# Spare matmuls with zero weights into an open PSUM accumulation, and a shorter window for the planner that places them

## Chip, cores, metric

One core of one Trainium2 chip. The metric is the device time of one execution in microseconds (us), median of the runs. The experiments ran in three sets, each on another chip, beside the kernel before on the same one.

## The reference

Two layers, each of multi-head attention and an MLP, on x of 2048 rows by 512, in bf16. Attention has 32 heads of 16; the MLP has 1792 hidden columns and a tanh gelu.

```python
x = x + A(layernorm(x), wqkv, wo)        # softmax(q k^T / 4) v, 32 heads of 16, then wo
x = x + B(layernorm(x), w1, b1, w2, b2)  # gelu(x w1 + b1) w2 + b2
x = x + A(layernorm(x), wqkv, wo)
x = x + B(layernorm(x), w1, b1, w2, b2)
```

## The kernel before

A Python planner runs before anything is compiled. It has a model of each engine's time, picks the next operation for each engine, and so fixes every engine's instruction order and its semaphores (the counters by which one engine waits for another). The 4096 score tiles (128 keys by 512 queries, one PSUM bank each) are the core of the work: ScalarE takes the exp of most of them, two or three banks at a time, VectorE approximates the exp of the rest, and TensorE multiplies the result with V ("PV") into bank 5, which stays open through a pass of the keys.

By its trace TensorE is idle for 199.6 of the 1629.9 us of the span, and its granted clock was 0.50 after windows of 3.41 us in which it had been idle. So the planner puts *spare matmuls* into gaps. Their results are never read. In the code below, shortened, `...` stands for what is cut, as is a guard in the `for` line.

```python
WINDOW = 3.4      # us over which the planner averages its estimate of TensorE's activity
WARM = 0.38       # below this average, a gap gets spare matmuls
...
    def fill(self, start, nxt):            # before TensorE's next operation, due at `start`
        while self.filler and self.mode:
            now = self.clock["pe"]
            mode = "F" if nxt.mode == self.mode == "F" else "P"
            into, back = ...               # the planner's cost of changing the tiling, 0.107 us each
            b, t = self.free(now, nxt.writes)   # which bank is free, and when
            now = max(now, t)
            if start - now < into + MM + back + FMARGIN or self.active(start) >= WARM:
                return
            op = self.filler(b, mode)      # four matmuls of 32 columns side by side: one group
            ...
    def free(self, now, ahead):
        best = (None, 1e9)
        for b in (6, 7, 0, 1, 2, 3, 4, 5):
            k = "B.%d" % b
            if k in ahead or not P.reads.get(k) and P.lastw.get(k) not in self.s.fills:
                continue                   # still holds a result that someone has to read
            t = ...                        # when its last reader is done
            if max(t, now) < max(best[1], now):
                best = (b, t)
        return best
```

So a gap gets nothing if no bank's last reader is done in time. The 0.107 us is a constant of the planner. In the trace before, a PV group starts 0.32 or 0.33 us after the score group ahead of it (329.75 and 330.08, 331.05 and 331.37), and 0.21 or 0.22 us after another PV group (330.09, 330.30, 330.52), so the change from one to the other took about 0.1 us there.

The softmax here doesn't subtract the row's maximum and nothing guards it: scores larger than these inputs give would overflow.

## Time and profile before

| | before |
|---|---|
| median of the first 3 runs | 1632.78 us |
| span in the profile | 1629.9 us |
| ScalarE busy / idle | 1560.7 / 69.2 us |
| mean granted TensorE clock, profiled run | 0.986 |
| windows of 3.41 us at half clock in that run | 13 |
| groups of spare matmuls | 174 on free banks |

ScalarE (ACT) is the bound: with the exps and the gelus above all it is busy for 96% of the span. What can be won lies in its idle time, and about half of that is the kernel's start and end. The lines that carry this are shown in the prediction.

### The profile page before, as it was taken

The page shows a single profiled execution, that of the slowest core. Times are in us where ns is not written, and L with a number is a line of the kernel's source. Part 1 is how long each engine was busy: PE and PEld are TensorE (multiplying, and loading weights), DVE is VectorE, ACT ScalarE, POOL GpSimd, SP SyncE. Part 2 cuts the span into 40 slices and gives each one's busy share as a digit, 9 for nine tenths or more (in the row PEclk, how much of TensorE's full clock was granted, in tenths as well). Part 3 has the DMA queues.
Part 4 walks back from the last instruction along what each step waited for, and adds up shares of the span by engine and source line. Part 5 has one row for each costly group of instructions (what it writes and reads, how often), then busy time and mean ns, then how long its engine had stood idle before and what let it go on. Part 6 is the DMA issues. An engine that isn't in the chain of part 4 may idle for free.

```text
span 1629.9 us, 32720 instructions
## 1 busy us (share of the span) xinstructions
PE 1430.3 (88%) x13701; PEld 418.1 (26%) x13838; DVE 1355.2 (83%) x2612; ACT 1560.7 (96%) x1402; POOL 111.6 (7%) x143
## 2 busy tenths in 40 slices
PE   6997888989898989899889989788898889888988
PEld 2222222222222222222222222222222222233434
DVE  6579999878887988987787788888888988897883
ACT  5999999999999999999998999989999999999995
POOL 3200000000000000000110001111000000000000
PEclk9999999999999999999999999999999999999999
DMA  5100001001010011100111001001101100010110
GB/s 173 22 1 1 1 14 34 27 4 39 25 33 27 1 27 40 34 27 1 27 46 47 7 14 40 2 1 27 46 11 30 34 14 11 17 40 24 50 53 27
DMA packets 88319, 44.85 MB, mean 28 GB/s; under 512 B 33645, under 2 KB 88174, under 8 KB 88174
## 3 DMA queue, kind: packets, MB, share of 16 engines
q1 hardware_dynamic: 88174, 42.75, 9.8%
q8 instruction: 111, 1.82, 0.5%
q14 instruction: 34, 0.28, 0.1%
HBM read 33.03 MB, written 2.10 MB: 22 GB/s over the span
## 4 chain that ended last, share of the span: by engine, by line
ACT 58%; PE 36%; DVE 3%; issue 1%; DMA 1%; POOL 0%; ACTq 0%
ACT pt L1360 49%; PE ps L1064 11%; PE ps L1421 11%; PE ps L868 4%; ACT v L1360 4%; PE ps L822 4%; PE ps L638 3%; ACT g L855 3%; ACT kt L1360 2%; PE ps L635 1%; DVE du L1209 1%; PE ps L749 1%; PE ps L1051 1%; ACT L855 1%; DMA xf<-xln 1%
## 5 line engine op out<-in xcount | busy, mean ns | idle before, releaser
L1360 ACT ACTIVATE pt<-ps 128x1024 bf16<-128x1024 f32 (+1 forms) x1217 | 1335.7, 1244 | 30.2 <-PE ps L1064 14.4
L1064 PE MATMUL ps<-qp,kt 32*128 32x512 bf16 x4096 | 545.5, 387 | 149.6 <-ACT pt L1360 109.5
L1209 DVE TENSOR_SCALAR du<-ps 128x512 uint16<-128x512 f32 x650 | 440.1, 685 | 112.7 <-PE ps L1064 106.2
L1421 PE MATMUL ps<-pt,v 128*17 128x512 bf16 (+1 forms) x3205 | 450.9, 364 | 2.3 <-ACT pt L1360 1.0
L1064 PEld LDWEIGHTS ps<-qp,kt 32*128 32x128 bf16 x4096 | 141.9, 91 | 700.6 <-ACT pt L1360 304.1
L1421 PE MATMUL ps<-du,vc 128*17 128x512 bf16 (+1 forms) x2178 | 305.1, 360 | 1.6 <-DVE du L1272 1.1
L1272 DVE TENSOR_SCALAR du<-du 128x2048 uint16<-128x2048 uint16 (+1 forms) x329 | 222.4, 681 | 2.5
L1028 POOL TENSOR_SCALAR qp<-q,mask 128x512 bf16<-128x512 bf16 (+1 forms) x92 | 68.7, 747 | 1273.0 <-PE ps L1064 1263.7
L1421 PE MATMUL ps<-du,v 128*17 128x512 bf16 (+1 forms) x726 | 140.3, 363 | 2.4 <-DVE du L1272 0.9
L1421 PEld LDWEIGHTS ps<-pt,v 128*17 128x17 bf16 x3205 | 107.6, 88 | 125.8 <-issue 96.7
L1270 DVE TENSOR_SCALAR du<-du 128x1024 uint16<-128x1024 uint16 (+1 forms) x329 | 136.6, 424 | 2.6
L868 PE MATMUL ps<-w,g 128*128 128x512 bf16 x404 | 118.5, 396 | 9.6 <-issue 5.7
L822 PE MATMUL ps<-xf,wr 128*128 128x512 bf16 (+1 forms) x427 | 111.0, 362 | 7.5 <-issue 5.6
L1360 ACT ACTIVATE v<-ps 128x1536 bf16<-128x1536 f32 (+1 forms) x77 | 102.6, 1354 | 4.0 <-PE ps L1421 2.0
L1421 PE MATMUL ps<-dh,vc 128*17 128x512 bf16 (+1 forms) x369 | 105.5, 360 | 0.1
L1421 PEld LDWEIGHTS ps<-du,vc 128*17 128x17 bf16 x2178 | 83.0, 89 | 58.5 <-issue 26.5
L836 DVE TENSOR_SCALAR g<-ps,hb1t 128x512 bf16<-128x512 f32 (+1 forms) x112 | 79.9, 713 | 16.8 <-PE ps L822 15.1
L1209 DVE TENSOR_SCALAR dh<-ps 128x512 uint16<-128x512 f32 x111 | 76.2, 686 | 12.1 <-PE ps L1064 9.2
L1209 DVE TENSOR_SCALAR kt<-ps 128x512 uint16<-128x512 f32 x98 | 67.3, 686 | 15.8 <-PE ps L1064 14.6
L1051 PE MATMUL ps<-w 128*32 128x512 bf16 x697 | 71.5, 398 | 1.8 <-DVE du L1209 1.6
L1360 ACT ACTIVATE kt<-ps 128x1536 bf16<-128x1536 f32 (+1 forms) x52 | 71.6, 1382 | 0.7 <-PE ps L1064 0.3
L1421 PE MATMUL ps<-kt,v 128*17 128x512 bf16 (+1 forms) x264 | 63.1, 365 | 0.1
(78 smaller groups left out, 1136.1 us busy)
## 6 DMA issues: line engine op xcount, KB each, us to landing
wr<-in_B_w_dram SPq DMA_DIRECT2D x59, 256.0 KB, 2.9
wr<-in_A_wqkv_dram SPq DMA_DIRECT2D x24, 256.0 KB, 2.8
wr<-in_A_wo_dram SPq DMA_DIRECT2D x18, 256.0 KB, 2.9
x<-in_A_x_dram SPq DMA_DIRECT2D x4, 512.0 KB, 8.5
out_dram<-x SPq DMA_DIRECT2D x16, 128.0 KB, 1.7
w<-in_B_w_dram SPq DMA_DIRECT2D x1, 1792.0 KB, 11.0
g<-in_A_wqkv_dram SPq DMA_DIRECT2D x3, 512.0 KB, 6.2
kt<-in_B_w_dram SPq DMA_DIRECT2D x4, 256.0 KB, 3.3
```

The source lines that it names most:

```text
L822: fns = [lambda e, dc=dc, j=j, pb=pb: e.matmul(pb, lhsT=T["WR"][w][:, 256 * dc + 128 * j:256 * dc + 128 * j + 128], rhs=T["XF"][:, dc, q], ...
L836: yield _Op("dve", 0.21 + n / 966, lambda e, fc=fc, pb=pb: e.tensor_scalar(T["G"][:, fc, q], pb, T["HB1T"][:, fc:fc + 1], None, op0=ALU.ad ...
L855: fns.append(lambda e, g=g: e.activation(out=g, in_=g, func=ACT.Gelu_apprx_tanh))
L868: fns = [lambda e, fc=fc: e.matmul(pb, lhsT=T["G"][:, fc, q], rhs=T["W2"][:, fc, :], start=(fc == 0), stop=False) for fc in range(NFC)]
L1028: yield _Op("pool", 0.1 + 0.6 * w / 512, lambda e, s=s, q=q, i=i, t=t, w=w: e.tensor_scalar(T["QP"][:, s, w * i:w * i + w], q, T["MASK"][: ...
L1051: fns.append(lambda e, o=o, a=a, m=m: e.matmul(o, lhsT=T["W2"][:, 0, m * a:m * a + m], rhs=T["W2"][:, 1, :], start=True, stop=True, tile_p ...
L1064: return (lambda e: e.matmul(o, lhsT=lhsT, rhs=rhs, start=True, stop=True, tile_position=(32 * a, 0)), ["K%d.%d.%d" % (l, gb, kt // 4), "Q ...
L1209: yield _Op("dve", 0.68, lambda e: e.tensor_scalar(u, self.bank(b), E_SCALE, E_BIAS, op0=ALU.mult, op1=ALU.add), reads=["B.%d" % b], write ...
L1270: yield _Op("dve", 0.08 + 0.14 * n, lambda e: e.tensor_scalar(U[:, 1, 0:n, :], U[:, 0, 0:n, :], SHIFT, None, op0=ALU.add), reads=key[0], w ...
L1272: yield _Op("dve", 0.08 + 0.28 * n, lambda e: e.tensor_scalar(U[:, 2:4, 0:n, :], U[:, 0:2, 0:n, :], 2 * SHIFT, None, op0=ALU.add), reads=k ...
L1360: yield _Op("act", 0.065 + 0.4267 * n, lambda e, src=src, dst=dst: e.activation(out=dst, in_=src, func=ACT.Exp, scale=0.25), reads=["B.%d" ...
L1421: op.fns.append(lambda e, o=o, lhsT=q[0][0][m], rhs=q[0][1][:, n * m:n * m + n], a=a, st=st, sp=sp: e.matmul(o, lhsT=lhsT, rhs=rhs, start= ...
```

## The change

The intent: when no free bank can be had at once, spare matmuls go to bank 5 in the midst of its accumulation, with weights of zero, which are meant to leave the sums as they are; and the planner averages activity over 2.5 us, so that shorter gaps are filled too.

```diff
-WINDOW = 3.4
+WINDOW = 2.5
@@ fill
             b, t = self.free(now, nxt.writes)
+            if b == PVB and mode == "F":
+                return
@@
-            self.fills.add(ev)
+            if b != PVB:
+                self.fills.add(ev)
@@ free
+        k = "B.%d" % PVB
+        if best[1] > now and self.pvopen and k not in ahead:
+            best = (PVB, 0.0)
         return best
@@ filler
+            if b == PVB:
+                o = self.bank(b)[m * a:m * a + 17, :]
+                fns.append(lambda e, o=o, a=a, m=m: e.matmul(o, lhsT=T["ZERO"][:, 0:17], rhs=T["W2"][:, 1, :],
+                                                             start=False, stop=False, tile_position=(0, m * a)))
+                continue
@@ pvs: after each PV operation is built
+                self.pvopen = all(begun) and all(self.pvleft[k] for k in cols)
(cut: the zero tile, its memset on GpSimd, and the field's first value)
```

The planner places a group in bank 5 only after each part of it has begun and while more is to come (`pvopen`).

More of the change, by code (lines that the diff above doesn't have):

```diff
@@ L447, in bass_interleave_layers__mha_block__dense_activation_gelu__prompt_kernel @@
         T["ONES1"] = sb([1, 128], BF16, "ones1")
+        T["ZERO"] = sb([128, 32], BF16, "zero")
         T["IDENT"] = sb([128, 128], BF16, "ident")
@@ L514, in init @@
         yield _Op("pool", 0.1, lambda e: e.memset(T["NHALF"][:], -0.5), writes=["NHALF"])
+        yield _Op("pool", 0.1, lambda e: e.memset(T["ZERO"][:], 0.0), writes=["ZERO"])
         yield _Op("pool", 0.1, lambda e: e.memset(T["ONES1"][:], 1.0), writes=["ONES1"])
@@ L1000, in setup_attention @@
         self.dmine = {c for q in self.dlist for c in q}
-        self.ended = False
+        self.ended, self.pvopen = False, False
         self.rush = self.base[(NL - 1, self.segs[-1][-3])]
@@ L1049, in filler @@
             m = 128 if mode == "F" else 32
+            if b == PVB:
+                o = self.bank(b)[m * a:m * a + 17, :]
+                fns.append(lambda e, o=o, a=a, m=m: e.matmul(o, lhsT=T["ZERO"][:, 0:17], rhs=T["W2"][:, 1, :], start=False,
+                                                             stop=False, tile_position=(0, m * a)))
+                continue
             o = self.bank(b)[m * a:m * a + m, :]
@@ L1052, in filler @@
                                                          stop=True, tile_position=(0, m * a)))
-        return _Op("pe", MM, fns, reads=["W2"], writes=["B.%d" % b], mode=mode)
+        return _Op("pe", MM, fns, reads=["W2"] + ["ZERO"] * (b == PVB), writes=["B.%d" % b], mode=mode)
     def score(self, cell, qs, bank):
```

## The prediction

> **What bounds the kernel now.** I read the table of busy time first, then the groups of instructions and the waits of ScalarE (ACT in the views), then busy time by short stretches, which gives the granted TensorE clock of each, and last TensorE's order of time inside one of them. Times are in us, means in ns.
>
> From the page, busy time and share of the span, and of its groups the exp and the spare matmuls:
>
> ```profile
> PE 1430.3 (88%) x13701; PEld 418.1 (26%) x13838; DVE 1355.2 (83%) x2612; ACT 1560.7 (96%) x1402; POOL 111.6 (7%) x143
> ...
> L1360 ACT ACTIVATE pt<-ps 128x1024 bf16<-128x1024 f32 (+1 forms) x1217 | 1335.7, 1244 | 30.2 <-PE ps L1064 14.4
> ...
> L1051 PE MATMUL ps<-w 128*32 128x512 bf16 x697 | 71.5, 398 | 1.8 <-DVE du L1209 1.6
> ```
>
> ACT is the bound. Its idle time is 1629.9 - 1560.7 = 69.2 us, all that any change of waits can win while ACT's work stays. L1051 is the helper of the spare matmuls: 696 of 32 columns, four to a group, so 174 groups (the 697th is a single wide one). Who ACT waits for:
>
> ```profile
> ACT kt L648 <- PE ps L638: 14.7, 2, 13.4
> ACT pt L1360 <- PE ps L1064: 14.4, 36, 1.3
> ACT pt L1360 <- PE ps L1421: 13.2, 11, 4.1
> ACT xf L602 <- PE ps L596: 7.4, 1, 7.4
> ACT g L831 <- PE ps L822: 3.3, 2, 2.6
> ```
>
> The first row is the start and the last two are the end of the kernel. Read by stretches, ACT idles 17.0 us in the first 50 us and 17.2 us in the last 30 us, where loading, the last transposes and the last layer set the pace and spare matmuls matter little. So about 35 us of idle lie in the 1550 us between: exps that wait for scores (L1064), or for room that PV (L1421) has to free.
>
> The clock explains part of that. Its mean over the run is 0.986. The record of the granted clock in the trace shows half speed in 11 places, nine of 3.41 us and two of 6.83 us: 9 x 3.41 + 2 x 6.83 = 44.4 us, or 13 windows of 3.41 us. TensorE loses half of that, 22 us of streaming. Four pairs of stretches, each 3.41 us before such a place and then the place itself; the columns are the length, busy us (instructions) of PE, weight loads, DVE, ACT, POOL, then the clock and DMA:
>
> ```profile
> 351.81:355.22 3.41, 1.97 (x20) 0.58 (x20) 3.04 (x6) 3.41 (x4) 0.00 (x0) 1.00 0.01 2
> 355.22:358.63 3.41, 3.41 (x26) 0.76 (x23) 3.17 (x9) 2.69 (x3) 0.00 (x0) 0.50 0.02 5
> 720.44:723.86 3.42, 1.75 (x14) 0.47 (x16) 0.69 (x1) 3.39 (x4) 0.00 (x0) 1.00 0.00 0
> 723.86:727.27 3.41, 3.41 (x15) 0.53 (x12) 2.76 (x5) 2.77 (x4) 0.00 (x0) 0.50 0.00 0
> 850.16:853.57 3.41, 2.11 (x23) 0.63 (x25) 3.41 (x10) 3.41 (x4) 0.00 (x0) 1.00 0.19 38
> 853.57:856.98 3.41, 3.41 (x23) 0.65 (x14) 2.23 (x6) 1.49 (x2) 0.00 (x0) 0.50 0.27 55
> 1010.59:1014.00 3.41, 1.86 (x27) 0.61 (x26) 3.05 (x7) 3.41 (x4) 0.00 (x0) 1.00 0.23 67
> 1014.00:1017.42 3.42, 3.42 (x27) 0.44 (x20) 2.79 (x5) 3.06 (x4) 0.00 (x0) 0.50 0.00 0
> ```
>
> The pattern: TensorE is idle for 1.3 to 1.7 of 3.41 us, the next window runs at 0.50, TensorE then has no idle at all, and ACT, full before, loses 0.72, 0.64, 1.92 and 0.36 us. Two of the four are what the change aims at: before 355 and 1014 no spare group was placed. In order of time, TensorE in the third pair:
>
> ```profile
> 853.18 1.95 PE L1051 MATMUL ps<-w 128*32 128x512 bf16 x16
> 855.06 0.61 PE L1064 MATMUL ps<-qp,kt 32*128 32x512 bf16 x3
> ```
>
> Here spare matmuls came just as the clock fell: 16 of them take 1.95 us ahead of the score, and the exps later wait 4.06 us for PV. A spare matmul in the wrong place costs more than it saves.
>
> [...] only 1.00 and 0.50 occur, in units of 3.41 us. [...] four spare matmuls of about 0.38 us latency each take 0.49 us together (1.95 / 4, partly at half clock), not four times one. [...]
>
> **The change, part by part.** I took counts from the two compiled instruction streams, no times.
>
> 1. *Spare groups on free banks.* The planner averages activity over 2.5 us instead of 3.4, so a short gap pulls the average below 0.38 sooner. Spare matmuls on banks go from 696 to 888: 174 to 222 groups, +48.
> 2. *Spare groups into the open PV bank.* 276 new matmuls with the zero tile, 69 groups. Together +117 groups. Start to start, groups in one run here are about 0.22 us apart at full clock (PV groups of four start at 330.09, 330.30, 330.52 in the trace). So +26 us of TensorE streaming against its 1629.9 - 1430.3 = 199.6 us of idle, nearly all in gaps.
> 3. *Does it come at the right places?* I counted groups by the running number of the score, which both streams share (4096). Ahead of the place at 355 there are 3 where none was, at 458 there are 2 for 0, at 649 there are 2 for 0. At 854 and 1014 there is still none; at 724, 792 and 1181 there are 0 for 1, 2 and 5, since the plan moved. Five of the 11 places follow a long gelu on ACT, during which scores stop for 6.27 us; they had 1 to 5 groups in the window already and still fell. I choose 13 to about 7 half-speed windows.
> 4. *Real work moved.* Scores stay 4096; exps of three banks go 546 to 539, of two 799 to 809, one of a single bank goes. At 1512 and 1084 ns (means by form) that is -10.6 + 10.8 - 0.6 = -0.4 us of ACT, nothing. DVE takes two more score cells; nothing. A memset of 128x32 on POOL, 7% busy, is nothing.
>
> The gain: over the 11 places plus the 5 us after each ACT idles 11.5 us. The background rate elsewhere in the middle, about 1.6%, would give 1.6 us in those 99 us, so some 10 us are due to the clock: the most that full removal could win. 6 of 13 windows removed: 10 x 6 / 13 = 4.6 us.
>
> The cost: each spare group stands in program order before a score and can delay it by up to 0.22 us. In the kernel before, ACT's idle in the spare runs and 1.5 us after them, outside the half-speed places, is about 5 us in 260 us, against 4.2 us at the background rate: under 0.01 us a group, so 117 groups cost about 1 us. The second of two score slots hides it. The sum: 1632.8 - 4.6 + 1 - 0.4 = 1628.8; I say 1628.5.
>
> **Rivals.** *The wait moves rather than goes.* The plan is reshuffled everywhere (2 more cells on DVE, other pairs, other half-speed places), and a single bad coincidence such as 854 costs 4 us. For it: the places at 854 and 1014 get no group. This makes -6 to +6 us on top, either way. *Spare matmuls become the delay.* TensorE is 88% busy by the view and fills 1.8% more; if every added group delayed a score that ACT waits for by 0.1 us, +12 us, about 1645. Against it: ACT waits for scores only 36 times in all. *Products with zero weights do not count as activity*, or PV into one bank in a row queues: then only the 48 bank groups help, and the gain is about 2 us, 1631. *All half-speed windows go*: 1632.8 - 10 + 1 = 1624. None of these reaches 2%, 32.7 us: faster by that would need nearly all of the 35 us of idle in the middle.
>
> **Range and chances.** The gain is capped at 10 us by the clock, and luck of the plan adds some 6 us either way; the bad side is a little longer by the delay rival. 1618 to 1641 should hold it 8 times in 10. Faster by over 2% 0.01, within 2% 0.97, slower 0.02.
>
> **What would show it.** In the profile after: 888 and 276 spare matmuls; PE busy up by some 25 us; mean clock up from 0.986 to about 0.993, so 5 to 9 windows at 0.50; ACT busy within 1 us of 1560.7, and its idle down to about 65 us, with the fall in the waits on L1064 and L1421. Wrong would be: a clock that does not rise though the groups are there (zero products or their places do not count); a clock near 1.00 and no gain (the spare work costs what the clock gave); or ACT idle that grows in new places beside the groups.

What is cut from it, where marked, are general statements about the clock, about matmuls side by side and about zero weights. "only 1.00 and 0.50 occur" is said of the granted clock, and the four spare matmuls that take 0.49 us together are those of the third pair. Groups of four start 0.22 us apart at clock 1.00 (nine groups at 705.72 in the run after take 2.13 us in all) and 0.43 us apart at 0.50 (853.64 and 854.07 in the run before). That zero weights leave the PV sums alone was the assumption; no run had shown it then.

## The result

| | before | after |
|---|---|---|
| median, 6 runs each | 1632.34 us | 1622.24 us (1618.27 to 1622.9) |
| ratio, 95% interval | | 0.9934 (0.9921 to 0.9947) |
| span in the profile | 1629.9 us | 1620.3 us |
| ScalarE busy / idle | 1560.7 / 69.2 us | 1558.2 / 62.1 us |
| clock, profiled run | 0.986 | 0.996 |
| windows of 3.41 us at half clock (one that begins in the last us of the run after is not counted) | 13 | 4 |

A ratio is the mean time of one kernel's fast runs over that of the other's of the same rounds, so it is not quite the ratio of the medians quoted.

The page of the changed kernel, busy time and the group of spare matmuls on free banks, which is L1064 here:

```profile
PE 1467.9 (91%) x14312; PEld 426.0 (26%) x14312; DVE 1355.9 (84%) x2616; ACT 1558.2 (96%) x1404; POOL 113.6 (7%) x144
...
L1064 PE MATMUL ps<-w 128*32 128x512 bf16 x889 | 82.7, 386 | 1.6 <-DVE du L1222 1.3
```

and, from the groups of all instructions, the new ones:

```profile
L1060 PE MATMUL ps<-w,zero 128*17 128x512 bf16 x276 | 26.6, 382 | 0.0
```

The counts are as planned (888 and one wide one, and 276). PE's busy time is not quite comparable: before, 13701 matmuls are on record beside 13838 weight loads, so 137 records are missing there; after, none. ScalarE's waits after (L1077 are scores, L1434 is PV):

```profile
ACT kt L653 <- PE ps L643: 15.4, 2, 13.5
ACT pt L1373 <- PE ps L1077: 12.0, 31, 0.8
ACT pt L1373 <- PE ps L1434: 8.3, 9, 2.6
ACT xf L607 <- PE ps L601: 7.4, 1, 7.4
ACT g L836 <- PE ps L827: 3.3, 2, 2.6
```

Start and end are as they were; waits for scores went from 14.4 to 12.0, waits for PV from 13.2 to 8.3 (the longest from 4.1 to 2.6, at another place). Of the 9.6 us of span, 7.1 are idle time and 2.5 are busy time.

How a spare group in the open bank does it is seen best where the prediction's first pair of stretches lay. TensorE in the order of time, before:

```profile
352.73 0.40 PE L1064 MATMUL ps<-qp,kt 32*128 32x512 bf16 x3 [0.29 <-ACT pt L1360]
353.06 0.38 PE L1421 MATMUL ps<-dh,vc 128*17 128x512 bf16 x1
353.06 0.38 PE L1421 MATMUL ps<-pt,v 128*17 128x512 bf16 x1
354.07 0.40 PE L1064 MATMUL ps<-qp,kt 32*128 32x512 bf16 x4 [0.63 <-DVE mv L567]
354.99 0.43 PE L1064 MATMUL ps<-qp,kt 32*128 32x512 bf16 x3 [0.52 <-ACT pt L1360]
355.35 1.02 PE L1421 MATMUL ps<-pt,v 128*17 128x512 bf16 x5
...
357.17 0.61 PE L1064 MATMUL ps<-qp,kt 32*128 32x512 bf16 x3
```

and the same work after:

```profile
352.98 0.39 PE L1077 MATMUL ps<-qp,kt 32*128 32x512 bf16 x3 [0.29 <-ACT pt L1373]
353.31 0.39 PE L1434 MATMUL ps<-dh,vc 128*17 128x512 bf16 x1
353.31 0.38 PE L1434 MATMUL ps<-pt,v 128*17 128x512 bf16 x1
353.32 0.81 PE L1060 MATMUL ps<-w,zero 128*17 128x512 bf16 x8
354.32 0.40 PE L1077 MATMUL ps<-qp,kt 32*128 32x512 bf16 x4 [0.20 <-DVE mv L572]
354.65 0.40 PE L1060 MATMUL ps<-w,zero 128*17 128x512 bf16 x4
355.24 0.39 PE L1077 MATMUL ps<-qp,kt 32*128 32x512 bf16 x3 [0.20 <-ACT pt L1373]
355.56 0.60 PE L1434 MATMUL ps<-pt,v 128*17 128x512 bf16 x5
...
356.50 0.39 PE L1077 MATMUL ps<-qp,kt 32*128 32x512 bf16 x3
```

Before, two gaps of 0.63 and 0.52 us stayed empty, the clock fell at 355.22, and the score at 357.17 took 0.61 where others take 0.40. After, three groups with zero weights stand in the same two gaps, nothing falls, and the three scores come at 356.50. As far as one trace each can show it, the groups do this: of two runs described below, e6, the changed kernel with only the groups in the open bank cut to one column, falls here again, and in the trace of e7, with only the other groups cut, I found no fall here. In e6, the stretch before the place and the place itself (columns as in the prediction):

```profile
352.71:356.12 3.41, 1.97 (x29) 0.76 (x29) 3.04 (x7) 3.41 (x4) 0.00 (x0) 1.00 0.01 2
356.12:362.95 6.83, 6.46 (x45) 1.54 (x47) 5.54 (x14) 5.71 (x6) 2.29 (x1) 0.50 0.00 1
```

What is left of half speed is mostly another kind. Stretches of the changed kernel: two windows ahead of a fall, each with the fall itself after it:

```profile
708.07:711.48 3.41, 1.12 (x6) 0.40 (x6) 0.00 (x0) 3.38 (x4) 0.00 (x0) 1.00 0.00 0
711.48:714.89 3.41, 3.41 (x14) 0.66 (x14) 0.00 (x0) 2.63 (x3) 0.00 (x0) 0.50 0.00 0
1008.44:1011.85 3.41, 1.83 (x23) 0.49 (x16) 3.23 (x6) 3.41 (x4) 0.80 (x1) 1.00 0.19 57
1011.85:1015.26 3.41, 3.41 (x25) 0.68 (x21) 2.59 (x5) 2.87 (x3) 0.00 (x0) 0.50 0.02 5
```

Three of the four (711, 1329, 1497) lie just after a pair of gelus of 6.27 us together on ScalarE, during which few scores are made (2, 2 and 3 of the 4096, where a stretch of that length has 16 on average); TensorE was idle for 2.3 us of the 3.41 before the first (nine spare groups stand at 705.7 to 707.9, just ahead of that window). The fourth is the place of the kernel before at 1014, for which the plan had no group.

### The profile page after: what moved, and what is told of

The parts are those of the page before. It is cut to its first block, busy times and chain, and to the rows that moved or that the text cites. A ratio compares the mean times of both kernels' runs of the same rounds, so it can differ in the third digit from the quotient of the medians.

```text
span 1620.3 us, 33812 instructions
## 1 busy us (share of the span) xinstructions
PE 1467.9 (91%) x14312; PEld 426.0 (26%) x14312; DVE 1355.9 (84%) x2616; ACT 1558.2 (96%) x1404; POOL 113.6 (7%) x144
## 4 chain that ended last, share of the span: by engine, by line
ACT 62%; PE 35%; DVE 2%; issue 1%; DMA 0%; POOL 0%; ACTq 0%
ACT pt L1373 51%; PE ps L1434 11%; PE ps L1077 11%; ACT v L1373 4%; PE ps L827 4%; PE ps L643 3%; PE ps L873 3%; ACT kt L1373 3%; ACT g L860 3%; PE ps L640 1%; PE ps L754 1%; ACT L860 1%; ACT L1373 1%; DVE du L1222 0%; PE ps L1064 0%
## 5 line engine op out<-in xcount | busy, mean ns | idle before, releaser
L1373 ACT ACTIVATE pt<-ps 128x1024 bf16<-128x1024 f32 (+1 forms) x1206 | 1320.2, 1247 | 23.3 <-PE ps L1077 12.0
L1077 PE MATMUL ps<-qp,kt 32*128 32x512 bf16 x4096 | 542.4, 384 | 126.7 <-ACT pt L1373 91.5
L1434 PE MATMUL ps<-pt,v 128*17 128x512 bf16 (+1 forms) x3157 | 434.3, 363 | 0.6 <-ACT pt L1373 0.5
L1077 PEld LDWEIGHTS ps<-qp,kt 32*128 32x128 bf16 x4096 | 142.3, 91 | 679.9 <-ACT pt L1373 284.5
L1434 PE MATMUL ps<-du,vc 128*17 128x512 bf16 (+1 forms) x2172 | 303.9, 358 | 0.4 <-ACT pt L1373 0.3
L1434 PE MATMUL ps<-du,v 128*17 128x512 bf16 (+1 forms) x724 | 138.5, 361 | 1.8 <-DVE du L1285 1.1
L1434 PEld LDWEIGHTS ps<-pt,v 128*17 128x17 bf16 x3157 | 103.5, 88 | 120.9 <-issue 95.8
L873 PE MATMUL ps<-w,g 128*128 128x512 bf16 x448 | 123.0, 385 | 2.9 <-ACT g L860 2.8
L827 PE MATMUL ps<-xf,wr 128*128 128x512 bf16 (+1 forms) x472 | 123.6, 365 | 1.1 <-DVE g L841 1.0
L1373 ACT ACTIVATE v<-ps 128x1536 bf16<-128x1536 f32 (+1 forms) x84 | 108.0, 1318 | 3.1 <-PE ps L1434 1.3
L1434 PE MATMUL ps<-dh,vc 128*17 128x512 bf16 (+1 forms) x378 | 107.7, 358 | 0.5 <-DVE du L1285 0.5
L1434 PEld LDWEIGHTS ps<-du,vc 128*17 128x17 bf16 x2172 | 83.0, 89 | 52.9 <-issue 22.1
L1064 PE MATMUL ps<-w 128*32 128x512 bf16 x889 | 82.7, 386 | 1.6 <-DVE du L1222 1.3
L1373 ACT ACTIVATE kt<-ps 128x1536 bf16<-128x1536 f32 (+1 forms) x58 | 82.6, 1430 | 0.7 <-PE ps L1077 0.4
L1434 PE MATMUL ps<-kt,v 128*17 128x512 bf16 (+1 forms) x287 | 77.5, 365 | 0.0
```

Source lines behind the costliest of these rows:

```text
L827: fns = [lambda e, dc=dc, j=j, pb=pb: e.matmul(pb, lhsT=T["WR"][w][:, 256 * dc + 128 * j:256 * dc + 128 * j + 128], rhs=T["XF"][:, dc, q], ...
L873: fns = [lambda e, fc=fc: e.matmul(pb, lhsT=T["G"][:, fc, q], rhs=T["W2"][:, fc, :], start=(fc == 0), stop=False) for fc in range(NFC)]
L1064: fns.append(lambda e, o=o, a=a, m=m: e.matmul(o, lhsT=T["W2"][:, 0, m * a:m * a + m], rhs=T["W2"][:, 1, :], start=True, stop=True, tile_p ...
L1077: return (lambda e: e.matmul(o, lhsT=lhsT, rhs=rhs, start=True, stop=True, tile_position=(32 * a, 0)), ["K%d.%d.%d" % (l, gb, kt // 4), "Q ...
L1373: yield _Op("act", 0.065 + 0.4267 * n, lambda e, src=src, dst=dst: e.activation(out=dst, in_=src, func=ACT.Exp, scale=0.25), reads=["B.%d" ...
L1434: op.fns.append(lambda e, o=o, lhsT=q[0][0][m], rhs=q[0][1][:, n * m:n * m + n], a=a, st=st, sp=sp: e.matmul(o, lhsT=lhsT, rhs=rhs, start= ...
```

## The experiments

Three tools made clean comparisons possible. First, the compiled streams showed that with the spare matmuls taken out there are just two orders of the real instructions among all variants but one (e12): that of the kernel before, called order A here, and that of the changed kernel, order B. They part at score 920 of 4096. PV groups alone leave order A as it was, to the instruction; the window of 2.5 us gives B, with PV groups or without. Windows of 2.6 to 3.2 us give A, 2.3 to 2.5 and 3.6 give B, 2.2 gives A again: which one comes out is chance, not a property of a short window. Second, a spare matmul can be cut to 1 column: the plan, the semaphores and the tiles stay, nearly all of the work goes. Third, each run reports its own mean clock, so time can be set against clock run by run. All were timed in five rounds beside the kernel before (four to six runs each); e1, e2, e3 and e5 shared one set of 11 runs of it, e4, e6, e8 and e9 a second, and the rest a third. All outputs are right.

| run | order | groups: banks + PV | clock, mean of its runs | median us | ratio (95%) |
|---|---|---|---|---|---|
| before (33 runs) | A | 174 + 0 | 0.9826 | 1633.21 | 1 |
| after | B | 222 + 69 | 0.9957 | 1622.24 | 0.9934 (0.9921 to 0.9947) |
| e1_window_only | B | 238 + 0 | 0.9860 | 1629.95 | 0.9979 (0.9947 to 1.0011) |
| e2_pv_only | A | 138 + 69 | 0.9946 | 1625.68 | 0.9951 (0.9939 to 0.9963) |
| e3_after_tiny | B | none whole | 0.9488 | 1655.47 | 1.0136 (1.0123 to 1.0149) |
| e5_before_tiny | A | none whole | 0.9454 | 1661.77 | 1.0164 (1.0147 to 1.0181) |
| e4_all_zero | B | 222 + 69, all zero | 0.9943 | 1622.14 | 0.9936 (0.9919 to 0.9953) |
| e6_tiny_pv | B | 222 + (69 cut) | 0.9858 | 1631.51 | 0.9984 (0.9965 to 1.0003) |
| e7_tiny_bank | B | (222 cut) + 69 | 0.9588 | 1647.23 | 1.0088 (1.0069 to 1.0106) |
| e8_window_2_6 | A | 161 + 89 | 0.9932 | 1627.76 | 0.9968 (0.9953 to 0.9982) |
| e9_warm_45 | A | 225 + 145 | 0.9960 | 1624.15 | 0.9945 (0.9931 to 0.9959) |
| e10_window_3_6 | B | 183 + 56 | 0.9928 | 1625.7 | 0.9949 (0.9926 to 0.9972) |
| e11_warm_42 | B | 258 + 93 | 0.9975 | 1619.83 | 0.9918 (0.9902 to 0.9933) |
| e12_warm_50 | own | 317 + 173 | 0.9978 | 1625.95 | 0.9957 (0.9941 to 0.9973) |

**The two halves of the change.** Edit of the first: the kernel before with

```diff
-WINDOW = 3.4
+WINDOW = 2.5
```

> Half of the change alone: the planner's window of 2.5 us, no spare matmuls into the PV bank; 238 groups on free banks (before 174, after 222 + 69). Theory A (what counts is that gaps are filled, by whichever group): 4 to 7 half-speed windows, ratio to before 0.994 to 0.998. Rival B (the PV bank is what closes the gaps, since no bank is free in those): clock stays near 0.986 to 0.989, ratio 0.998 to 1.002.

Measured: 0.9979, and the interval holds 1. The same instructions ran between 1620.79 and 1638.7 us, at clocks from 0.994 down to 0.978: three runs at 1624.4 or less, three at 1635.5 or more and none between, a spread that is more than the whole change brings. The profiled run is the slowest, with 21 half-speed windows. The ratio alone would suit either theory; the mean clock, 0.9860, speaks for rival B: 64 more groups on banks alone do not lift the clock reliably.

Edit of the second: the changed kernel with

```diff
-WINDOW = 2.5
+WINDOW = 3.4
```

> The other half alone: spare matmuls into the PV bank, window left at 3.4 us; 138 groups on free banks and 69 into PV, 207 in all. Theory A (number of gaps filled): 7 to 10 half-speed windows, ratio 0.996 to 0.999. Rival B (the PV bank does it): clock 0.993 or more, ratio 0.994 to 0.996.

Measured: 0.9951 at clock 0.9946 with 207 groups in all, fewer than the 238 of the other half. The profiled run had 6 half-speed windows against 13. Rival B again: where the group can be placed counts, not only how many there are. As order A is kept here, this gain is that of the 69 PV groups, net of 36 groups on banks that gave way to them (174 to 138).

**Clock or order?** Edit of the third, in the changed kernel, and of the fourth, the same for the one form of spare matmul in the kernel before:

```diff
-                o = self.bank(b)[m * a:m * a + 17, :]
+                o = self.bank(b)[m * a:m * a + 17, 0:1]
-                ... lhsT=T["ZERO"][:, 0:17], rhs=T["W2"][:, 1, :]
+                ... lhsT=T["ZERO"][:, 0:17], rhs=T["W2"][:, 1, 0:1]
-            o = self.bank(b)[m * a:m * a + m, :]
+            o = self.bank(b)[m * a:m * a + m, 0:1]
-            ... rhs=T["W2"][:, 1, :], start=True
+            ... rhs=T["W2"][:, 1, 0:1], start=True
```

> The changed kernel's plan to the instruction, but every spare matmul has 1 column instead of 512 (it stays in place with its tile and semaphores, and does next to no work). It tells the clock from the reshuffled plan. Theory A (the gain is the clock that the spare work keeps up): many more half-speed windows than the kernel before, 25 or more, mean clock below 0.975, ratio to before 1.005 to 1.02. Rival B (the gain is the luck of another plan): clock falls, but the time stays within 0.3% of the changed kernel, ratio 0.991 to 0.997.

> The kernel before, plan to the instruction, with its 696 spare matmuls cut to 1 column. Theory A: half-speed windows rise from 13 to 20 or more and the time by 0.3 to 1.5%. Rival (spare matmuls delay scores as much as the clock gives): within 0.2% of before though the clock falls. Taken with the same cut in the changed kernel: if the two bare plans differ by less than 0.2%, the plan itself is no part of the gain; if the changed plan is 0.4% or more faster bare, it is.

Measured: without the spare work the changed kernel takes 1655.47 us and the one before 1661.77, at clocks of 0.9488 and 0.9454. Theory A holds: with 51 and 53 half-speed windows in the profiled runs, the spare work is worth 33 us in the changed kernel (1655.5 - 1622.2) and 29 us in the one before (1661.8 - 1633.2; its 1.64% is above the 1.5% expected at most). That is net of the time the spare matmuls take on TensorE (busy 71.5 us in the kernel before, 82.7 and 26.6 in the changed one), as the cut takes away 511 of their 512 columns. ScalarE's waits of the bare changed kernel show where it bites:

```profile
ACT pt L1373 <- PE ps L1077: 35.2, 62, 1.4
...
ACT pt L1373 <- PE ps L1434: 12.2, 9, 4.0
```

Waits for scores are 35.2 us there against 12.0 with the spare work. For the order the pair decides nothing: bare, B is faster by 6.3 us by the medians but 5.2 by the means (the ratios differ by 0.28%, between the two limits set), and at a clock that is 0.0034 higher too, worth 2.6 us by the slope found below.

**Which groups?** Edits: only the first two pairs of lines above (PV groups cut), and only the last two (bank groups cut).

> The changed kernel to the instruction, with only the 276 spare matmuls into the PV bank cut to 1 column; the 222 groups on free banks stay. If those 69 PV groups are what closes the gaps that no free bank could (theory P): clock 0.975 to 0.988, ratio 0.997 to 1.003, as with the shorter window alone. If the 222 groups on banks carry it: clock 0.992 or more, ratio 0.993 to 0.996.

> The changed kernel to the instruction, with the 222 groups on free banks cut to 1 column and only the 69 PV groups left whole. With all cut the ratio was 1.0136 at clock 0.947, with PV cut alone 0.9984 at 0.984. If each group, of whichever bank, is worth the same, 69 of 291 groups give a quarter of the way from 1.0136 to 0.9934: 1.009, clock 0.958. If PV groups stand where the need is greatest, more: 1.006 or less, clock 0.965 or more.

Measured: without the 69 PV groups the changed kernel is back at 0.9984 and clock 0.9858, with 15 half-speed windows in the profiled run instead of 4. With them alone it stands at 1.0088 and 0.9588. The PV groups add 0.010 of clock both ways (0.9957 - 0.9858, and 0.9588 - 0.9488), 0.00014 a group; the 222 bank groups add 0.037 (0.9858 - 0.9488), 0.00017 a group. So in this one plan a group is worth nearly the same in either bank, and the first theory of the run without bank groups was right. What the open bank gives is more places that can be filled. Waits for scores with the PV groups cut, from the view of ScalarE's waits:

```profile
ACT pt L1373 <- PE ps L1077: 18.8, 43, 1.0
...
ACT pt L1373 <- PE ps L1434: 10.1, 9, 2.6
```

18.8 us against 12.0 with them.

**Do zero weights count as activity?** Edit, in the changed kernel, for the groups on free banks:

```diff
-            ... lhsT=T["W2"][:, 0, m * a:m * a + m], rhs=T["W2"][:, 1, :]
+            ... lhsT=T["ZERO"][:, 0:32] if m == 32 else T["W2"][:, 0, 0:128], rhs=T["W2"][:, 1, :]
-        ... reads=["W2"] + ["ZERO"] * (b == PVB)
+        ... reads=["W2", "ZERO"]
```

> The changed kernel to the instruction, but the spare matmuls on free banks too have zero weights, so all 291 groups multiply by zero. Theory Z1 (activity is counted by what runs, whatever the data): clock 0.994 to 0.997 and ratio to before 0.992 to 0.996, as the changed kernel. Theory Z0 (products with zero count less): the clock falls well below, to 0.985 or less, and the ratio goes to 0.998 or more.

Measured: 1622.14 us, 0.9936, clock 0.9943 (runs of 0.990 to 0.997, those of the changed kernel 0.994 to 0.997). Theory Z1: 291 groups with zero weights hold the clock as those with real weights do. The streamed operand stayed as it was, so only zero weights are tested.

**Window or order?** Edits: the window at 2.6 us, which gives order A, and at 3.6 us, which gives order B.

> The changed kernel with a window of 2.6 us in place of 2.5: the order of the real instructions is then that of the kernel before (up to the last few us), with 161 groups on banks and 89 into PV. It tells the window from the order. If the order that the 2.5 us window happens to give is worth 3 to 6 us (theory O): ratio 0.9945 to 0.9965, as PV groups alone with the long window (0.9951). If the shorter window's groups are worth it (theory W): ratio 0.992 to 0.994, as the changed kernel.

> The changed kernel with a window of 3.6 us: the order of the real instructions is then that of the changed kernel, with 183 groups on banks and 56 into PV, 239 in all. If the order is what gives the few us beside the PV groups (theory O): ratio 0.993 to 0.995 at clock 0.994 or more. If the shorter window's groups do it (theory W): ratio 0.996 to 0.999.

Measured: 0.9968 for A with the short window, 0.9949 for B with the long one. A short window with PV groups is no better than PV groups with the long one (0.9951, same order; e8's 0.9968 lies just outside the range that theory O gave, on the slow side), and order B without the short window keeps part of the gain, though at a clock of 0.9928, below what theory O asked. Neither interval is narrow enough alone, so I put all runs together. Over the 86 runs of orders A and B with whole bank groups (33 of before, 6 of after and those of e1, e2, e4, e6, e8 to e11), the least-squares fit of time on clock and order is

time = 1620.5 + 0.77 x (1 - clock) x 1000 - 1.7 if order B,

with a bootstrap 95% interval of 0.70 to 0.82 for the slope and 0.9 to 2.6 us for the order; the residual is 1.4 us. The interval takes runs as independent; but whole kernels lie up to 1.9 us off the line (e8), and drawing kernels in place of runs widens the order's interval to 0.2 to 3.3. The 33 runs of the kernel before alone give a slope of 0.79, so this is not made by comparing kernels. For the window's own groups nothing is left that the fit can see. Why order B is faster at one clock was not taken apart; two of its differences are 7 fewer exps of three banks for 10 more of two. The waits point to PV: ScalarE's exps wait for it for 11.5 to 11.8 us in the profiles of order A with PV groups (e2, e8, e9), for 8.3 to 10.2 in those of order B (after, e4, e10, e11). So most of the fall from 13.2 to 8.3 seems to belong to the order and not to the clock; it is partly paid back in waits for scores (before, at 0.986, 14.4 for scores and 13.2 for PV; e6, order B at 0.984, 18.8 and 10.1).

**A better one?** Edits: the changed kernel with the activity goal WARM = 0.38 raised to 0.45, 0.42 and 0.50.

> The changed kernel with the activity goal at 0.45 in place of 0.38: order of the kernel before, 225 groups on banks and 145 into PV, 370 in all. If only gaps count and the clock is nearly full already: clock 0.997 or more, 0 to 2 half-speed windows, ratio 0.991 to 0.994. If more spare work now delays scores: clock the same, but ACT idle and the ratio rise, 0.995 to 1.0.

> Search for a better one: the changed kernel's order with the activity goal at 0.42 in place of 0.38, 258 groups on banks and 93 into PV. Clock 0.997 or more and ratio 0.991 to 0.993 if the last 4 or 5 half-speed windows can be filled; 0.993 to 0.995 if they lie under the long gelus, where no group fits or helps, or if added groups delay as much as they save.

> Too much of it: activity goal 0.50, 317 groups on banks and 173 into PV, 490 in all, in an order of its own from score 1713 on. Clock 0.997 or more. If spare groups cost nothing: ratio 0.990 to 0.993. If they start to delay scores: waits of ACT for scores rise by 3 us or more and the ratio is 0.994 to 1.0.

Measured: 0.42 gives 1619.83 us, 0.9918, the best of all and ahead of both kernels: its profiled run has a clock of 0.999 with one half-speed window left, and waits for scores of 8.1 us. Against the changed kernel it is 2.4 us by the medians of different rounds, and the two intervals overlap, so that it beats the changed kernel is likely and not shown. 0.45 met neither of its forecasts (clock 0.9960, ratio 0.9945, between the two ranges); it comes out in order A and is where the fit puts it (1623.6 by the fit, 1624.05 measured mean). 0.50 has clock 0.9978 and is yet slower, 1625.95. Its waits of ScalarE are not those that I expected:

```profile
ACT pt L1373 <- PE ps L1434: 17.0, 14, 3.0
...
ACT pt L1373 <- PE ps L1077: 9.5, 29, 0.9
```

Waits for scores did not rise; waits for room that PV frees doubled against the changed kernel's 8.3. As this plan has an order of its own, whether the added groups or the order put PV late is open.

## Why the prediction was right in kind, and where its sizes were off

The way from spare groups to clock to ScalarE's waits was right; the gain was 10.1 us where 4.3 were forecast. The result lies inside the range because that allowed some 6 us for the luck of the plan, of which the plan gave 1.7; the rest came from the clock, which the forecast had too small.

- *What bounds the kernel.* Right. ScalarE's idle fell and so did the time; only waits in the middle moved.
- *"The pattern" of four pairs* was a choice among 11 places. Over all of them TensorE's idle time in the window before was 1.08 to 1.66 us, and in three (648, 904, 1181) ScalarE lost 0.06 us or less within the place; in four TensorE was idle within the place. Idle time is a strong sign and no rule: in the window-only run (e1), whose trace lacks no record, 13 falls follow windows with 0.91 to 2.00 us idle, while 6 windows with 1.35 to 1.72 us were not followed by a fall.
- *"A spare matmul in the wrong place costs more than it saves"*, read from the wait of 4.06 us near 854, does not hold as put. The same exp, in the same order, waits 3.08 us with every spare matmul cut (e5, at half speed there) and 2.43 to 2.67 us at full clock with them (e2, e8, e9). Most of that wait is the order's.
- *Steps 1 and 2, the counts.* Right to the instruction: 888 and 276 on record.
- *Step 3, how many half-speed windows go.* This is the term that was mis-sized. "I choose 13 to about 7": 4 are left in the profile, so 9 went, not 6, and the clock was 0.996, not 0.993. Counting groups by score number named the new ones at 355, 458 and 649 and the bare place at 1014 well (it fell again), but places at 792, 854 and 1181, with no group just ahead, went as well. A place of half speed is not fixed: identical instructions ran at clocks from 0.978 to 0.994 (window alone), so one trace of falls cannot be ticked off one by one.
- *"10 x 6 / 13 = 4.6 us."* The rate behind it comes out: 13 windows, some 22 us of streaming lost, were to be worth 10 us, 0.45 us for each; the fit says 0.77 us per 0.001 of clock, which is 0.77 / 1.63 = 0.47 us per us of streaming lost. Some of the agreement is luck, as the 10 us hold the 4.06 us near 854, of which some 2.5 do not go with the clock. And the base was one lucky run: the kernel before runs at 0.9826 on average, not at the profiled 0.986, and falls by 0.0131 to be made good. 13.1 x 0.77 = 10.1 us, plus 1.7 us for the order, is 11.8 us, against 11.7 us between the means (1633.4 and 1621.6, of different rounds); the fit was made with these runs, so this is a summing up and no test. For the pair of profiles: 10 x 0.77 + 1.7 = 9.4 us of the 9.6 measured.
- *"The most that full removal could win" being 10 us* was accordingly too low a cap on the whole change: nearly all of it was reached at 0.996, and 1620 us at 0.9975 went past it.
- *The cost, "117 groups cost about 1 us".* No sign of it in the fit up to 370 groups: the kernels with 351 and 370 lie 0.8 us below and 0.4 us above it. But it is not refuted: the kernels with 291, 174 and 222 groups cut (e3, e5, e7) lie 2.7, 1.8 and 2.6 us below the line continued to their clocks, some 0.01 us for each group, as forecast; a line that bends would look the same. The reading behind it, 5 us of idle in 260 us, comes to 4.4 us in 195 when read again (the places and the 5 us after them left out), with the same result.
- *Step 4, moved work, -0.4 us of ScalarE.* Busy time fell by 2.5 us. The means by form that I multiplied count the overlap of neighbours twice. From the starts and ends in the trace, an exp that follows without idle adds 1346 ns (three banks) or 917 ns (two) of busy time, one that follows idle time 1451 or 1024: some 105 ns more for each wait. 7 exps fewer and 10 more are -9.4 + 9.2 = -0.2 us, the lost one of a single bank -0.5, and eleven waits fewer of exps (124 before, 113 after) -1.2 us; that makes 1.9 of the 2.5.
- *Rivals.* "Products with zero weights do not count": refuted (e4). "Spare matmuls become the delay": not in this change; open for 490 groups. "The wait moves" by a reshuffled plan, plus or minus 6 us: an effect of that kind exists, but by the fit it is 1.7 us, in favour; PV groups alone left the order as it was, and the 2.5 us window changed it.

## What to carry to other kernels

Here TensorE was not the bound but fed the bound in bursts; its mean clock was 0.9454 (the kernel before) and 0.9488 (the changed one) without the spare work, 0.9826 and 0.9957 with it, and the times fell by 29 and 33 us. Where a spare group lacked a bank, the open accumulation took its zero products without harm: in ten experiments the results stayed correct. In a kernel of this shape both are worth a try. Judge such work by mean clock and time over several runs, not by one trace: one set of instructions (e1) differed by 0.016 of mean clock and 18 us between runs. And where a planner decides, first cut the added work to nothing in place: it parts the work's effect from that of another order.
